# Decode attention for two problems on one core: the last rows of wo as one stripe in three pieces

## The chip, the cores and the metric

The kernel runs on one core of a Trainium2 chip. The metric is the device time of one execution in microseconds (us). The kernel before took 363.1 us (median of 3 runs, 363.03 to 363.24).

## The reference

Two independent problems, A and B, of the same shape. Each has 2 batches, one query token, 32 query heads on 16 key/value heads of 128 elements, and attends to the last 4096 of 16384 cached positions.

```python
q = (x @ wq).reshape(B, Sq, Hq, Dh)            # x 2x1x576, wq 576x4096
k = repeat(k_cache[:, :, Sk - W:, :], 2)       # W = 4096, Dh = 128
v = repeat(v_cache[:, :, Sk - W:, :], 2)
p = softmax(q k^T * Dh ** -0.5)
out = (p v).reshape(B, Sq, Hq * Dh) @ wo       # wo 4096x576
# result: concatenate([out_A, out_B], axis=-1), 2x1x1152, bf16
```

All inputs are bf16. Almost all of the bytes are the cached keys and values: 32 slabs of 4 MB.

## The kernel before, in words

**Stream.** All large loads go through SP's queue in one fixed order, written as the list `stream` (L322). A slab is the K or the V of one batch for four key/value heads: 128 partitions of 32 KB, each partition holding 128 keys (`KJ`) of 128 elements. There are 16 K slabs (K0 to K15) and 16 V slabs (V0 to V15); V comes three slabs behind K (`LAG`). They share a ring of four slots. A slot is loaded again when the last reader of its slab is done. The output matrix wo has a buffer of its own, `wob`, of 16 rows of 576 elements per partition.

**Groups.** Two slabs, one for each batch, make a group G of 4 key/value heads (0 to 7; 0 to 3 are problem A, `NG` is 8). For each group DVE transposes K (L436), TensorE makes the scores (L462 and L266, a helper that issues a matmul without loading weights), DVE, GpSimd and TensorE find the maxima, ScalarE takes the exponentials (L500), DVE transposes them (L509), TensorE multiplies by V (L539, 32 matmuls per slab, four at a time in four column groups), and DVE scales and folds the result (L562 to L569).

**Dg and pick.** What is left has to become the stationary side of the projection. `make_dg` (L573) spreads it over partitions by one fp32 matmul with a 0/1 matrix, and `make_pick` (L582) multiplies by a mask and sums over the entries that are zero but for one (L590 or L597, then L606). For groups 0 to 5 the 0/1 matrix is `selm`: an even group fills partitions 0 to 63 of `oM`, an odd one 64 to 127, so that two groups together make 16 sets of weights with all 128 partitions (16 rows of wo each, a stripe, called M0 to M2). For the last two groups, 6 and 7, the matrix is `selx` and the mask `cm16`: each group fills all 128 partitions of `oP` with 8 sets of weights, and each has 8 rows of wo of its own, called W6 and W7.

**Projection.** `make_projm` (L622) multiplies a stripe, `make_proj` (L645) the 8 rows of one of the last groups. For problem B each row is four matmuls of 144 columns (`cells`, L616): two column halves `c` by two halves `h`, the latter in two column groups of the array. The result is summed in PSUM (`PJ`).

**The end.** After the loop over the slabs (L741 to L770) the order on each engine is written out by hand. M2's 16 rows are multiplied in parts of 8, 4 and 4, put between other work. V15 is loaded in two parts, keys 0 to 79 and 80 to 127 (`v_cuts`, L160); the first part's matmuls run while the second is on its way. W6 comes in one DMA of 1152 KB, which waits for the first 8 rows of M2's projection; W7 in three, of 4, 3 and 1 rows (`w_cuts`, L162), which wait for all of M2's projection, since they go to the second half of `wob`. `filler` (L389) issues matmuls whose result nobody reads. Group 7's dg and pick are made for batch 0 (slab V14) and batch 1 (V15) apart. Then come W6's 8 rows, W7's rows 0 to 3, 4 to 6, and the last row, whose weights are loaded ahead (L654) and whose column half 0 is finished before half 1, so that DVE (L687) and ScalarE (L688) each evict one half and SP and ScalarE issue one output DMA each (L694).

The order at the end of the kernel before:

```python
        make_projm(NM - 1, 12, 16)
        filler(4)
        make_evac(i + 2)
        make_PV(i + 3, (0,))
        make_dg(NG - 1, (0,))
        make_pick(NG - 1, (0,))
        filler(4)
        make_PV(i + 3, (1,))
        make_evac(i + 3)
        filler(3)
        make_dg(NG - 1, (1,))
        make_pick(NG - 1, (1,))
        make_proj(NG - 2)
        make_proj(NG - 1)
        make_E(NPROB - 1)
```

Of the kernel before, what the change touches and what calls it, by code (L numbers as in the profile page):

```python
# [63 lines left out]
def build_kernel(nc, probs, out):  # L64
# [17 lines left out]
    KJ = W // 32  # L82
# [11 lines left out]
    with es:  # L94
# [21 lines left out]
        cm16 = sb("cm16", [128, 16], FP32)  # L116
        jmask_f = sb("jmask_f", [128, 8], FP32)
        m8 = sb("m8", [128, 16, 8], FP32)
        selx = sb("selx", [128, 8, 16], FP32)
# [13 lines left out]
        oP = sb("oP", [128, 2, 8, Bb], BF16)  # L133
        oM = sb("oM", [128, 16, Bb], BF16)
# [25 lines left out]
        v_cuts = [0, 80, KJ]  # L160
        lastv_sem = [sem("lastv")]
        w_cuts = [0, 4, 7, 8]  # L162
# [77 lines left out]
        d_cm = mask(cm16[:, 0:16], ident_f[:].rearrange("p (x q) -> p q x", q=16), AX.X, "cm16")  # L240
# [6 lines left out]
        p_sx = pool(lambda e: e.tensor_copy(selx[:], jmask_f[:, 0:8].unsqueeze(2).broadcast_to([128, 8, 16])), [d_jf], "selx")  # L247
# [83 lines left out]
        stream.append(("W", NG - 2))  # L331
        stream.append(("W", NG - 1))
        NM = NG // 2 - 1
# [13 lines left out]
        projm_first = {}  # L347

        def issue(key):
            kind, i = key  # L350
            if kind in "MW":
                n = 16 if kind == "M" else 8
                first_g = 2 * i if kind == "M" else i
                P, gl = first_g // GP, first_g % GP
                at = 0 if kind == "M" else 8 * (i % 2)
                rows = probs[P][4][gl * 1024:gl * 1024 + 128 * n, :].rearrange("(p j) n -> p j n", j=n)
                deps = ([projm_op[i - 1]] if i >= 1 else []) if kind == "M" else [projm_first[NM - 1] if i == NG - 2 else projm_op[NM - 1]]
                cuts = [(0, n, wo_sem[i % 2])]
                if i == NG - 1:
                    cuts = [(w_cuts[k], w_cuts[k + 1], ([wo_sem[1]] + lastw_sem)[k]) for k in range(3)]  # L360
                stream_dma[key] = []
                for j0, j1, sm in cuts:
                    def f(e, j0=j0, j1=j1, sm=sm):
                        return e.dma_start(wob[:, at + j0:at + j1, :].rearrange("p j n -> p (j n)"),
                                           rows[:, j0:j1, :].rearrange("p j n -> p (j n)")).then_inc(sm, 16)
                    stream_dma[key].append((j0, j1, dma_op("sp", sm, 1, f, deps, "wo%d_%d" % (i, j0))))
                return
            P, g, b = i // (2 * GP), (i // 2) % GP, i % 2
            src_t = probs[P][1] if kind == "K" else probs[P][2]
            src = src_t[b, 4 * g:4 * g + 4, Sk - W:Sk, :].rearrange("k (r j) d -> r k j d", j=KJ)  # L370
            r = slot_of[key]
            prior = uses[r][:uses[r].index(key)]
            deps = [last_reader[prior[-1]]] if prior else first_deps[r]
            cuts = [(0, KJ, ring_sem[r])]
            if key == ("V", NSLAB - 1):
                cuts = [(v_cuts[k], v_cuts[k + 1], ([ring_sem[r]] + lastv_sem)[k]) for k in range(2)]
            stream_dma[key] = []
            for c0, c1, sm in cuts:
                def f(e, c0=c0, c1=c1, sm=sm):
                    return e.dma_start(ring[:, r, c0 * 128:c1 * 128],  # L380
                                       src[:, :, c0:c1, :].rearrange("r k j d -> r k (j d)")).then_inc(sm, 16)
                stream_dma[key].append((c0, c1, dma_op("sp", sm, 1, f, deps, "%s%d_%d" % (kind, i, c0))))
# [23 lines left out]
        proj_op = {}  # L406
# [166 lines left out]
        def make_dg(G, bs=(0, 1)):  # L573
            b0, nb = bs[0], len(bs)
            sl_, p_sl = (selx, p_sx) if G >= NG - 2 else (selm, p_sm)
            n, bank, op = tb_job(lambda e, bank: e.matmul(bank[:, 0:128 * nb], sl_[:].rearrange("p h c -> p (h c)"),
                                                          oR[:, b0:b0 + nb, :].rearrange("p b d -> p (b d)"), start=True, stop=True),
                                 "dg%d_%d" % (G, b0), [ch[(G, "red%d" % b)] for b in bs] + [p_sl])
            ch[(G, "dg")] = op
            dg_job[(G, bs)] = (n, bank)  # L580

        def make_pick(G, bs=(0, 1)):  # L582
            v = G % 2
            b0, nb = bs[0], len(bs)
            n, bank = dg_job[(G, bs)]
            tv = tmp[:, 0:128 * nb]
            if G < NG - 2:
                h0 = 64 * v
                tv = tmp[h0:h0 + 64, 0:256]
                a = dve(lambda e: e.tensor_tensor(  # L590
                    tv.rearrange("p (b c j) -> p b c j", b=2, c=8), bank[h0:h0 + 64, 0:256].rearrange("p (b c j) -> p b c j", b=2, c=8),
                    jmask_f[h0:h0 + 64, 0:8].unsqueeze(1).unsqueeze(3).broadcast_to([64, 2, 8, 16]), ALU.mult),
                    [ch[(G, "dg")], d_jf, ch["tmp"]], "A%d" % G)
                dst, q = oM[h0:h0 + 64, :, :].rearrange("p j b -> p b j"), G // 2
                free, c = [projm_op[q - 1]] if q >= 1 else [], 8
            else:
                a = dve(lambda e: e.tensor_tensor(  # L597
                    tv.rearrange("p (b c j) -> p b c j", b=nb, c=16), bank[:, 0:128 * nb].rearrange("p (b c j) -> p b c j", b=nb, c=16),
                    cm16[:, 0:16].unsqueeze(1).unsqueeze(3).broadcast_to([128, nb, 16, 8]), ALU.mult), [ch[(G, "dg")], d_cm, ch["tmp"]], "A%d" % G)
                dst = oP[:, v, :, b0:b0 + nb].rearrange("p j b -> p b j")  # L600
                free, c = [], 16
            tb_consumer[n] = a

            def f_pick(e):
                with nc.allow_low_precision(reason="one term of the c is not zero"):
                    return e.tensor_reduce(dst, tv.rearrange("p (b c j) -> p b j c", b=nb, c=c), AX.X, ALU.add)  # L606
            ch[(G, "oP", b0)] = dve(f_pick, [a] + free, "oP%d_%d" % (G, b0))
            ch["tmp"] = ch[(G, "oP", b0)]
# [12 lines left out]

        def make_projm(q, j0=0, j1=16):  # L622
            P, start = 2 * q // GP, (2 * q) % GP == 0 and j0 == 0
            ensure(("M", q))
# [13 lines left out]
            deps = [ch[(2 * q, "oP", 0)], ch[(2 * q + 1, "oP", 0)], stream_dma[("M", q)][0][2]]  # L638
            if start:
                deps += [e_ops[(P - 1, 0)], e_ops[(P - 1, 1)]] if P >= 1 else [q_ev[2]]  # L640
            projm_op[q] = pe(f, deps, "projm%d_%d" % (q, j0))
            if j0 == 0:
                projm_first[q] = projm_op[q]

        def make_proj(G):  # L645
            v = G % 2
            ensure(("W", G))
            oPs = [ch[(G, "oP", b)] for b in range(2) if (G, "oP", b) in ch]
            for j0, j1, dma in stream_dma[("W", G)]:
                held = G == NG - 1 and j1 == 8  # L650
                if held:
                    def f_w(e):
                        for h in range(2):
                            last = e.add_instruction(mybir.InstLdweights(  # L654
                                name=nc.get_next_instruction_name(), engine=mybir.EngineType.PE,
                                ins=[e.lower_ap(oP[:, v, 7, :], for_matmul_weights=True)], outs=[],
                                tile_size=(128, 32), tile_position=(0, 32 * h)))
                        return last
                    pe(f_w, oPs, "projw%d" % G)

                    for c in range(2):
                        def f_c(e, c=c):
                            for h in range(2):
                                last = cell(e, oP[:, v, 7, :], 8 * v + 7, c, h, False, True)
                            return last
                        last_cell[c] = pe(f_c, oPs + [dma], "proj%d_7%d" % (G, c))
                    continue

                def f(e, j0=j0, j1=j1):
                    for j in range(j0, j1):  # L670
                        last = cells(e, oP[:, v, j, :], 8 * v + j, False)
                    return last
                proj_op[G] = pe(f, oPs + [dma], "proj%d_%d" % (G, j0))

        def make_E(P):
# [7 lines left out]
            for h in range(2):  # L683
                def f_first(e, h=h):
                    return e.dma_start(out[:, 0, h * NH:(h + 1) * NH], out_sb[:, h * NH:(h + 1) * NH]).then_inc(out_sem, 16)
                dma_op(("sp", "act")[h], out_sem, 1, f_first, [e_ops[(0, 0)], e_ops[(0, 1)], stream_dma[("W", NG - 1)][1][2]], "out0_%d" % h)
# [61 lines left out]
        make_projm(NM - 1, 0, 8)  # L748
        make_dg(NG - 2)
        make_projm(NM - 1, 8, 12)  # L750
# [5 lines left out]
        make_projm(NM - 1, 12, 16)  # L756
# [5 lines left out]
        filler(4)  # L762
# [5 lines left out]
        make_proj(NG - 2)  # L768
        make_proj(NG - 1)
# [93 lines left out]
```

## Time and profile before

| what | value |
|---|---|
| time, median of 3 runs | 363.1 us |
| time of the profiled execution | 363.1 us |
| its span (first to last instruction) | 361.8 us |
| bytes read from HBM | 153.10 MB, 423 GB/s over the span |
| busy: TensorE (PE), DVE, ScalarE (ACT), GpSimd (POOL) | 229.0, 218.6, 45.4, 24.3 us |
| mean granted clock of TensorE | 0.887 of full speed |
| last V matmul, second part of V15 | issued from 354.20 us on |
| W6's first row, W7's first row, last row | 357.10, 358.50, 359.82 us |
| evictions, output DMAs issued | 360.10 and 360.15, 360.46 and 360.47 us |

Times inside the execution are counted from the start of the span. The profiled execution took 1.3 us more than its span. In a timeline line the first number is the start, the second the duration, then engine, line, operation, output and inputs, count, and in brackets the idle time before it with what ended it. PEld is the loading of weights, SPq and ACTq are the issue of a DMA.

### The profile page before, as it was taken

The numbers are of one execution on the slowest core, as the hardware profiler recorded it, in microseconds if no ns is written. First come the engines' busy times: TensorE is split into PE (matmuls) and PEld (weight loads), VectorE is DVE, ScalarE is ACT, GpSimd is POOL, SyncE is SP. The second block draws the span as 40 slices with busy tenths as digits, with TensorE's granted clock in tenths as the row PEclk, the third lists the DMA queues.
The fourth block names the chain that finished last, engine by engine and source line by source line (L and its number), as shares of the span: only waits on it lengthen the run. The fifth ranks groups of instructions, "written<-read, shape, count | busy, mean of one in ns | idle before, by whom it ended". The sixth has DMA issues, their size and how long they took to land.

```text
span 361.8 us, 2701 instructions
## 1 busy us (share of the span) xinstructions
PE 229.0 (63%) x1357; PEld 56.1 (16%) x943; DVE 218.6 (60%) x150; ACT 45.4 (13%) x77; POOL 24.3 (7%) x84
## 2 busy tenths in 40 slices
PE   0397687767464866671696656662776675667575
PEld 0010111112110211120121211110112121112222
DVE  0811898495949392924919493952927776675522
ACT  1002100040031002200005000500005000500500
POOL 4200101100010001000010000000010000001000
PEclk9999698969999889888798998899589897869989
DMA  8999999999999999999999999999999999999996
GB/s 327 449 428 420 442 426 424 446 413 446 417 447 420 442 422 422 439 438 420 438 424 434 431 438 412 448 420 442 424 435 429 428 438 420 434 442 420 427 417 258
DMA packets 6088, 153.28 MB, mean 424 GB/s; under 512 B 684, under 2 KB 828, under 8 KB 1084
## 3 DMA queue, kind: packets, MB, share of 16 engines
q1 hardware_dynamic: 6056, 153.10, 98.7%
q8 instruction: 9, 0.15, 0.2%
q14 instruction: 3, 0.02, 0.0%
q10 hardware_dynamic: 20, 0.01, 0.0%
HBM read 153.10 MB, written 0.00 MB: 423 GB/s over the span
## 4 chain that ended last, share of the span: by engine, by line
DMA 49%; DVE 24%; PE 16%; issue 8%; ACT 1%; POOL 1%; SPq 0%
DMA ring<-in_B_k_cache_dram 25%; DVE xt L436 15%; DMA ring<-in_B_v_cache_dram 9%; DMA ring<-in_B_wq_dram 7%; DMA ring<-in_A_k_cache_dram 6%; PE st L266 6%; PE st L462 5%; DMA wob<-in_B_wo_dram 3%; DVE oR L569 2%; DVE mx L470 2%; DVE pT L509 2%; PE pj L266 2%; DVE tmp L562 2%; PE ot L539 1%; ACT pR L500 1%
## 5 line engine op out<-in xcount | busy, mean ns | idle before, releaser
L462 PE MATMUL st<-xt,zq 128*128 128x512 bf16 x256 | 119.3, 466 | 93.6 <-DVE xt L436 93.6
L436 DVE STREAM_TRANSPOSE xt<-ring 128x4096 f32<-128x4096 f32 x32 | 141.6, 4429 | 33.5 <-DMA ring<-in_A_k_cache_dram 18.2
L266 PE MATMUL st<-xt,zq 128*128 128x512 bf16 x256 | 118.0, 461 | 0.0
L500 ACT ACTIVATE pR<-st,bias 128x512 bf16<-128x512 f32 x32 | 40.0, 1419 | 219.0 <-DVE bias L493 219.0
L462 PEld LDWEIGHTS st<-xt,zq 128*128 128x128 bf16 x256 | 28.3, 110 | 211.5 <-DVE xt L436 110.0
L539 PE MATMUL ot<-ring,pT 128*32 128x512 bf16 x512 | 32.0, 393 | 8.3 <-DMA ring<-in_B_v_cache_dram 8.3
L493 DVE SCALAR_TENSOR_TENSOR bias<-vmask,tb,offm 128x4 f32<-128x4 f32 x8 | 1.8, 224 | 37.1 <-PE tb L490 37.1
L523 DVE TENSOR_REDUCE ssum<-tb 128x2 f32<-128x8 f32 x8 | 1.3, 162 | 33.4 <-PE tb L520 33.4
L428 POOL TENSOR_TENSOR zq<-qs,bmask 128x64 bf16<-128x64 bf16 x32 | 8.6, 292 | 161.2 <-PE st L266 140.3
L509 DVE STREAM_TRANSPOSE pT<-pR 128x2048 bf16<-128x2048 bf16 x8 | 18.4, 2303 | 0.7 <-ACT pR L500 0.7
L562 DVE SCALAR_TENSOR_TENSOR tmp<-ot,rsb,dmask 128x512 f32<-128x512 f32 x16 | 11.5, 719 | 9.4 <-PE ot L539 9.4
L281 PE MATMUL ot<-ring,pT 128*32 128x512 bf16 x18 | 7.6, 421 | 15.1 <-DMA ring<-in_A_wq_dram 14.5
L539 PEld LDWEIGHTS ot<-ring,pT 128*32 128x32 bf16 x512 | 12.4, 99 | 23.7 <-DMA ring<-in_B_v_cache_dram 10.5
L569 DVE TENSOR_REDUCE oR<-tmp 128x128 f32<-128x512 f32 x15 | 15.6, 1039 | 0.5
L266 PE MATMUL pj<-ring,pT 128*32 128x512 bf16 x36 | 12.1, 422 | 0.0
L266 PE MATMUL pj<-wob,oM 128*2 128x288 bf16 (+1 forms) x64 | 10.2, 256 | 0.0
L470 DVE TENSOR_REDUCE mx<-st 128x2 f32<-128x1024 f32 x8 | 9.7, 1208 | 0.1
L500 ACT ACTIVATION_READ_ACCUMULATOR pR<-st,bias 128x1 f32 x32 | 9.1, 283 | 0.0
L636 PE MATMUL pj<-wob,oM 128*2 128x288 bf16 x32 | 7.9, 286 | 0.0
L224 DVE TENSOR_TENSOR xt<-xt,hmask 4x1152 bf16<-4x1152 bf16 x2 | 2.8, 1398 | 8.4 <-DMA xt<-in_A_x_dram 8.4
L266 PE MATMUL st<-ring,pT 128*32 128x512 bf16 x18 | 7.4, 414 | 0.0
L472 POOL TENSOR_TENSOR mv<-mx,v 128x2 f32<-128x2 f32 x8 | 1.6, 195 | 80.0 <-DVE mx L470 80.0
(71 smaller groups left out, 79.5 us busy)
## 6 DMA issues: line engine op xcount, KB each, us to landing
ring<-in_A_k_cache_dram SPq DMA_DIRECT2D x8, 4096.0 KB, 24.9
ring<-in_A_v_cache_dram SPq DMA_DIRECT2D x8, 4096.0 KB, 30.0
ring<-in_B_k_cache_dram SPq DMA_DIRECT2D x8, 4096.0 KB, 28.5
ring<-in_B_v_cache_dram SPq DMA_DIRECT2D x7, 4096.0 KB, 31.8
ring<-in_A_wq_dram SPq DMA_DIRECT2D x1, 4608.0 KB, 13.6
ring<-in_B_wq_dram SPq DMA_DIRECT2D x1, 4608.0 KB, 24.1
wob<-in_A_wo_dram SPq DMA_DIRECT2D x2, 2304.0 KB, 29.8
ring<-in_B_v_cache_dram SPq DMA_DIRECT2D x1, 2560.0 KB, 26.9
```

The lines of the kernel that those rows point to most:

```text
L266: return e.add_instruction(mybir.InstMatmult(name=nc.get_next_instruction_name(), engine=mybir.EngineType.PE, ins=[e.lower_ap(mv_), e.lowe ...
L281: last = e.matmul(QB[c], wt, mv_, start=first, stop=True, skip_group_check=True)
L428: last = e.tensor_tensor(dst, src, msk, ALU.mult)
L436: Xop[(t, jh)] = dve(lambda e: e.transpose(xt[:, jh, :].bitcast(FP32).rearrange("p (kp x kt) -> p x kp kt", kp=2, kt=2), ring[:, r, jh * H ...
L462: last = e.matmul(ob, wt, mv_, start=first, stop=True, skip_group_check=True)
L470: ch[(G, "max")] = dve(lambda e: e.tensor_reduce(mx[:], st[:, :].rearrange("p (x t) -> p t x", t=2), AX.X, ALU.max), [Sop[(2 * G + 1, 1)]] ...
L500: last = e.activation(pR[:].rearrange("p (x k) -> p k x", k=4)[:, kv, :], st[:, :].rearrange("p (x t) -> p t x", t=2)[:, kv % 2, :], ACTF.Exp,
L509: pT_op[G] = dve(lambda e: e.transpose(pT[:, v, :].rearrange("p (w j q) -> p j w q", w=4, q=8), pR[:].rearrange("p (j w q) -> p j w q", w= ...
L539: last = e.matmul(OTB[32 * c:32 * c + 32, :], pT[:, v, base + 32 * c:base + 32 * c + 32], ring[:, r, jj * 128:(jj + 4) * 128], start=rd == ...
L562: evac_op[i] = dve(lambda e: e.scalar_tensor_tensor(tv, o, rsb[:, v, b:b + 1], dm, ALU.mult, ALU.mult), deps, "ev%d" % i)
L569: ch[(G, "red%d" % b)] = dve(lambda e: e.tensor_reduce(oR[:, b, :], tmp[:].rearrange("p (j d) -> p d j", j=4), AX.X, ALU.add), [evac_op[i] ...
L636: last = e.matmul(PJ[0], oM[:, j, :], mv_, start=start and j == 0, stop=True, skip_group_check=True)
```

## The change

- Groups 6 and 7 are picked like all others, with `selm` and the 64-partition form, into the halves of one set of weights; `selx`, `cm16` and `oP` go, and with them one copy on GpSimd and one reduction on DVE near the start.
- wo's last 16 rows per partition are one stripe M3 in three DMAs of 12, 3 and 1 rows (1728, 432 and 144 KB). Each piece waits for the rows of M2 that it overwrites: the first for M2's rows up to 12, the others for all of M2.
- `oM` has two buffers, by the parity of the stripe; a pick waits for the projection two stripes back.
- The projection of the last 16 rows, in groups of 12, 3 and 1, stands behind the last pick; every group waits for all picks of groups 6 and 7 and for its own piece.
- V15 is divided at key 96 instead of 80: parts of 3072 and 1024 KB, 24 and 8 matmuls.
- Fillers: 2 instead of 4 between the two parts of V15, and 4 new ones between group 7's last dg and the projection.

The diff, cut to its core:

```diff
-        oP = sb("oP", [128, 2, 8, Bb], BF16)
-        oM = sb("oM", [128, 16, Bb], BF16)
+        oM2 = [sb("oM%d" % k, [128, 16, Bb], BF16) for k in range(2)]
...
-        v_cuts = [0, 80, KJ]
+        v_cuts = [0, 96, KJ]
-        w_cuts = [0, 4, 7, 8]
+        m_cuts = [0, 12, 15, 16]
...
-        d_cm = mask(cm16[:, 0:16], ident_f[:].rearrange("p (x q) -> p q x", q=16), AX.X, "cm16")
...
-        p_sx = pool(lambda e: e.tensor_copy(selx[:], jmask_f[:, 0:8].unsqueeze(2).broadcast_to([128, 8, 16])), [d_jf], "selx")
...
-        stream.append(("W", NG - 2))
-        stream.append(("W", NG - 1))
-        NM = NG // 2 - 1
+        NM = NG // 2
+        stream.append(("M", NM - 1))
...
-                deps = ([projm_op[i - 1]] if i >= 1 else []) if kind == "M" else [projm_first[NM - 1] if i == NG - 2 else projm_op[NM - 1]]
-                cuts = [(0, n, wo_sem[i % 2])]
-                if i == NG - 1:
-                    cuts = [(w_cuts[k], w_cuts[k + 1], ([wo_sem[1]] + lastw_sem)[k]) for k in range(3)]
+                cuts = [(0, 16, wo_sem[i % 2])]
+                if i == NM - 1:
+                    cuts = [(m_cuts[k], m_cuts[k + 1], ([wo_sem[1]] + lastw_sem)[k]) for k in range(3)]
...
+                    deps = [projm_rows[i - 1][j1]] if i >= 1 else []
...
-            sl_, p_sl = (selx, p_sx) if G >= NG - 2 else (selm, p_sm)
...
+            h0, q = 64 * v, G // 2
+            tv = tmp[h0:h0 + 64, 0:128 * nb]
+            a = dve(lambda e: e.tensor_tensor(
+                tv.rearrange("p (b c j) -> p b c j", b=nb, c=8), bank[h0:h0 + 64, 0:128 * nb].rearrange("p (b c j) -> p b c j", b=nb, c=8),
+                jmask_f[h0:h0 + 64, 0:8].unsqueeze(1).unsqueeze(3).broadcast_to([64, nb, 8, 16]), ALU.mult),
+                [ch[(G, "dg")], d_jf, ch["tmp"]], "A%d_%d" % (G, b0))
+            dst = oM2[q % 2][h0:h0 + 64, :, b0:b0 + nb].rearrange("p j b -> p b j")
+            free = [projm_rows[q - 2][16]] if q >= 2 else []
...
             deps = [ch[(2 * q, "oP", 0)], ch[(2 * q + 1, "oP", 0)], stream_dma[("M", q)][0][2]]
+            if q == NM - 1:
+                deps = oPs_last() + [dma for c0, c1, dma in stream_dma[("M", q)] if c0 <= j0 and j1 <= c1]
...
-        make_projm(NM - 1, 12, 16)
+        make_projm(NM - 2, 12, 16)
         filler(4)
         make_evac(i + 2)
         make_PV(i + 3, (0,))
         make_dg(NG - 1, (0,))
         make_pick(NG - 1, (0,))
-        filler(4)
+        filler(2)
         make_PV(i + 3, (1,))
         make_evac(i + 3)
         filler(3)
         make_dg(NG - 1, (1,))
         make_pick(NG - 1, (1,))
-        make_proj(NG - 2)
-        make_proj(NG - 1)
+        filler(4)
+        make_projm(NM - 1, 0, 12)
+        make_projm(NM - 1, 12, 15)
+        make_last_row()
         make_E(NPROB - 1)
```

`make_last_row` is the last row's part of the old `make_proj`, with row 15 of the stripe and `oM`'s weights: load the weights ahead, then column half 0, then half 1.

More of the change, by code (lines that the diff above doesn't have):

```diff
@@ L115, in build_kernel @@
         dmask = sb("dmask", [128, 4], FP32)
-        cm16 = sb("cm16", [128, 16], FP32)
         jmask_f = sb("jmask_f", [128, 8], FP32)
         m8 = sb("m8", [128, 16, 8], FP32)
-        selx = sb("selx", [128, 8, 16], FP32)
         selm = sb("selm", [128, 16, 8], FP32)
@@ L346, in build_kernel @@
         projm_op = {}
-        projm_first = {}
+        projm_rows = {}
         def issue(key):
             kind, i = key
[L351 to L356, printed above, removed]
-                deps = ([projm_op[i - 1]] if i >= 1 else []) if kind == "M" else [projm_first[NM - 1] if i == NG - 2 else projm_op[NM - 1]]
-                cuts = [(0, n, wo_sem[i % 2])]
-                if i == NG - 1:
-                    cuts = [(w_cuts[k], w_cuts[k + 1], ([wo_sem[1]] + lastw_sem)[k]) for k in range(3)]
+            if kind == "M":
+                P, gl = 2 * i // GP, 2 * i % GP
+                rows = probs[P][4][gl * 1024:gl * 1024 + 2048, :].rearrange("(p j) n -> p j n", j=16)
+                cuts = [(0, 16, wo_sem[i % 2])]
+                if i == NM - 1:
+                    cuts = [(m_cuts[k], m_cuts[k + 1], ([wo_sem[1]] + lastw_sem)[k]) for k in range(3)]
                 stream_dma[key] = []
@@ L363, in f @@
                     def f(e, j0=j0, j1=j1, sm=sm):
-                        return e.dma_start(wob[:, at + j0:at + j1, :].rearrange("p j n -> p (j n)"),
+                        return e.dma_start(wob[:, j0:j1, :].rearrange("p j n -> p (j n)"),
                                            rows[:, j0:j1, :].rearrange("p j n -> p (j n)")).then_inc(sm, 16)
+                    deps = [projm_rows[i - 1][j1]] if i >= 1 else []
                     stream_dma[key].append((j0, j1, dma_op("sp", sm, 1, f, deps, "wo%d_%d" % (i, j0))))
@@ L405, in build_kernel @@
         evac_op = {}
-        proj_op = {}
         last_cell = {}
@@ L574, in make_dg @@
             b0, nb = bs[0], len(bs)
-            sl_, p_sl = (selx, p_sx) if G >= NG - 2 else (selm, p_sm)
-            n, bank, op = tb_job(lambda e, bank: e.matmul(bank[:, 0:128 * nb], sl_[:].rearrange("p h c -> p (h c)"),
+            n, bank, op = tb_job(lambda e, bank: e.matmul(bank[:, 0:128 * nb], selm[:].rearrange("p h c -> p (h c)"),
                                                           oR[:, b0:b0 + nb, :].rearrange("p b d -> p (b d)"), start=True, stop=True),
-                                 "dg%d_%d" % (G, b0), [ch[(G, "red%d" % b)] for b in bs] + [p_sl])
+                                 "dg%d_%d" % (G, b0), [ch[(G, "red%d" % b)] for b in bs] + [p_sm])
             ch[(G, "dg")] = op
@@ L585, in make_pick @@
             n, bank = dg_job[(G, bs)]
[L586 to L601, printed above, removed]
+            h0, q = 64 * v, G // 2
[6 more added lines that the diff above has]
+            free = [projm_rows[q - 2][16]] if q >= 2 else []
             tb_consumer[n] = a
@@ L605, in f_pick @@
                 with nc.allow_low_precision(reason="one term of the c is not zero"):
-                    return e.tensor_reduce(dst, tv.rearrange("p (b c j) -> p b j c", b=nb, c=c), AX.X, ALU.add)
+                    return e.tensor_reduce(dst, tv.rearrange("p (b c j) -> p b j c", b=nb, c=8), AX.X, ALU.add)
             ch[(G, "oP", b0)] = dve(f_pick, [a] + free, "oP%d_%d" % (G, b0))
@@ L620, in cells, with oPs_last @@
             return last
+        def oPs_last():
+            return [ch[(G, "oP", b)] for G in (NG - 2, NG - 1) for b in range(2) if (G, "oP", b) in ch]
         def make_projm(q, j0=0, j1=16):
             P, start = 2 * q // GP, (2 * q) % GP == 0 and j0 == 0
+            oM = oM2[q % 2]
             ensure(("M", q))
@@ L641, in make_projm @@
             projm_op[q] = pe(f, deps, "projm%d_%d" % (q, j0))
[L642 to L671, printed above, removed]
@@ new lines, in make_projm, with make_last_row, f_w, f_c @@
+            for k in range(j0 + 1, j1 + 1):
+                projm_rows.setdefault(q, {})[k] = projm_op[q]
+        def make_last_row():
+            q = NM - 1
+            oM = oM2[q % 2]
+            def f_w(e):
+                for h in range(2):
+                    last = e.add_instruction(mybir.InstLdweights(
+                        name=nc.get_next_instruction_name(), engine=mybir.EngineType.PE,
+                        ins=[e.lower_ap(oM[:, 15, :], for_matmul_weights=True)], outs=[],
+                        tile_size=(128, 32), tile_position=(0, 32 * h)))
+                return last
+            pe(f_w, oPs_last(), "projw")
+            for c in range(2):
+                def f_c(e, c=c):
+                    for h in range(2):
+                        last = cell(e, oM[:, 15, :], 15, c, h, False, True)
@@ L672, in f @@
                     return last
-                proj_op[G] = pe(f, oPs + [dma], "proj%d_%d" % (G, j0))
+                last_cell[c] = pe(f_c, oPs_last() + [stream_dma[("M", q)][2][2]], "proj15_%d" % c)
         def make_E(P):
@@ L685, in f_first @@
                     return e.dma_start(out[:, 0, h * NH:(h + 1) * NH], out_sb[:, h * NH:(h + 1) * NH]).then_inc(out_sem, 16)
-                dma_op(("sp", "act")[h], out_sem, 1, f_first, [e_ops[(0, 0)], e_ops[(0, 1)], stream_dma[("W", NG - 1)][1][2]], "out0_%d" % h)
+                dma_op(("sp", "act")[h], out_sem, 1, f_first, [e_ops[(0, 0)], e_ops[(0, 1)], stream_dma[("M", NM - 1)][1][2]], "out0_%d" % h)
             evs = [dve(lambda e: e.tensor_copy(out_w[:, 0:NQ], PJW[0]), [last_cell[0]], "E%d_0" % P),
@@ L747, in build_kernel @@
         make_evac(i + 1)
-        make_projm(NM - 1, 0, 8)
+        make_projm(NM - 2, 0, 8)
         make_dg(NG - 2)
-        make_projm(NM - 1, 8, 12)
+        make_projm(NM - 2, 8, 12)
         make_pick(NG - 2)
```

## The prediction

> **What bounds the kernel now.** I read the slices of the page first, then the chain that ended last, then the DMA issues and the timeline of the last 12 us, and last the busy time by clock window. First the page: share of the 16 DMA engines and GB/s in 40 slices of 9 us.
>
> ```profile
> DMA  8999999999999999999999999999999999999996
> GB/s 327 449 428 420 442 426 424 446 413 446 417 447 420 442 422 422 439 438 420 438 424 434 431 438 412 448 420 442 424 435 429 428 438 420 434 442 420 427 417 258
> ```
>
> Only the first and the last slice have room: the kernel is one stream of 153 MB, and only the start and the end can move. The end is on the chain (start us, us, what):
>
> ```profile
> 348.51 10.90 DMA wob<-in_B_wo_dram
> 359.41 0.04 issue
> 359.45 0.23 PE pj L614 x2
> ...
> 360.13 0.02 issue
> 360.15 0.28 ACT out_w L688
> ```
>
> The last-but-one piece of wo lands at 359.41, its three rows follow 0.04 us later, then the last row, the eviction and the two output DMAs. So PE has almost nothing left to do when the stream ends. The last pieces of the stream (KB, then us from issue to landing):
>
> ```profile
> ring<-in_B_v_cache_dram SPq DMA_DIRECT2D x1, 2560.0 KB, 26.9
> ring<-in_B_v_cache_dram SPq DMA_DIRECT2D x1, 1536.0 KB, 30.0
> wob<-in_B_wo_dram SPq DMA_DIRECT2D x1, 1152.0 KB, 19.4
> wob<-in_B_wo_dram SPq DMA_DIRECT2D x1, 576.0 KB, 10.2
> wob<-in_B_wo_dram SPq DMA_DIRECT2D x1, 432.0 KB, 10.9
> wob<-in_B_wo_dram SPq DMA_DIRECT2D x1, 144.0 KB, 10.8
> ```
>
> With the issues in SP's timeline (323.59, 324.2, 337.54, 348.13, 348.51, 349.0) they land at 350.5, 354.2, 356.94, 358.33, 359.41 and 359.8. The two largest gaps give the price of the stream: 1152 KB in 2.74 us and 576 KB in 1.39 us, 2.4 ns per KB. Now PE behind them:
>
> ```profile
> 350.51 1.26 PE L539 MATMUL ot<-ring,pT 128*32 128x512 bf16 x20 [1.45 <-DMA ring<-in_B_v_cache_dram]
> ...
> 354.20 0.83 PE L539 MATMUL ot<-ring,pT 128*32 128x512 bf16 x12 [1.14 <-DMA ring<-in_B_v_cache_dram]
> ...
> 357.10 0.23 PE L614 MATMUL pj<-wob,oP 128*2 128x144 bf16 x2
> ...
> 358.03 0.23 PE L266 MATMUL pj<-wob,oP 128*2 128x144 bf16 x2
> 358.47 0.43 PEld L614 LDWEIGHTS pj<-wob,oP 128*2 128x2 bf16 x8 [0.47 <-issue]
> 358.50 0.23 PE L614 MATMUL pj<-wob,oP 128*2 128x144 bf16 x2 [0.24 <-DMA wob<-in_B_wo_dram]
> ```
>
> The reader is to see that the first eight rows (group 6, whose pick was done long before) run from 357.10 to 358.1, while their successor's stripe is still in flight. Rows start at 358.50, 358.62, 358.75, 358.87: 0.124 us per row of four matmuls.
>
> **The change, part by part.**
>
> *Bytes and DMAs.* The same 2304 KB of wo come as 1728, 432 and 144 KB instead of 1152, 576, 432 and 144; the last V slab as 3072 and 1024 KB instead of 2560 and 1536. Nothing is added to the stream. The 1728 KB land when the 576 KB did, 358.33, less what one DMA costs by itself. That cost is not a row: from 1152 to 576 KB the price per KB is equal (saving 0); the 432 KB took 1.08 us against 1.04 at 2.4 ns per KB, so 0.04; twice that, 0.1, is my far end. I take 0.05 us: landing 358.28. The later pieces move with it.
>
> *SP's queue.* The 1728 KB wait for row 12 of the stripe before, not row 8: issued after PE's rows at 339.08 to 339.6 instead of at 337.54. What is queued behind it on SP waited for the rows at 347.44 to 348.0 anyway. At 340 the queue still holds over 14 us of work (354.2 lands before it), so the later issue is covered; if that cover were gone it would cost its 2.1 us.
>
> *Projection.* This is the term that counts. Groups 6 and 7 share one stripe, so each row's weights are half from each group and no row can start before the last pick. Eight rows that ran in the shadow (357.10 to 358.1) now stand behind it, and behind the landing of the 1728 KB. The landing is the later of the two (pick below). Before: rows 0-3 at 358.50, a wait of 0.29 us, rows 4-6 at 359.45, the last row at 359.82, DVE's eviction at 360.10. After: first row 0.15 us behind the landing (today's 576 KB: 358.50 against 358.33, 0.17; the 432 KB: 359.45 against 359.41, 0.04; the first is nearer, since it too waits for two semaphores): 358.43. Sixteen rows without a gap: the last starts 15 x 0.124 = 1.87 us later, 360.30. The pieces of 432 and 144 KB (359.36, 359.7) land while PE is in rows 7 to 10 and stop nothing. Eviction 0.28 us behind the last row's start, as now: 360.58 against 360.10, **+0.48**. Two more waits on semaphores that are long up: between the three rows and the last one today the pitch stays 0.06 us per pair, so 0; up to 0.1 each if PE can't look ahead.
>
> *Last V slab.* 512 KB more in the first part: it lands 512 x 2.4 ns = 1.23 us later, 351.7. The second ends where it did, 354.2, with 8 matmuls behind it instead of 12: 4 x 0.054 (20 in 1.26 us, less the 0.2 that a last one takes to drain) = 0.21 us less. The pick today ends at 357.53 + 0.39 = 357.92, so then 357.71, 0.6 us ahead of the landing: worth nothing.
>
> *Picks.* They go from 128 partitions (L597 292 ns, L606 386 ns for 128 elements) to 64 partitions with 16 outputs of 8 instead of 8 of 16. For 256 elements the two forms stand at 422 and 582 ns against 425 and 612: equal. No cost, and 0.6 us of cover.
>
> *Fillers.* Two fewer between the parts of V, four more behind the last dg. dg starts at 356.47, dg and the four take 0.42 + 4 x 0.216 us, to about 357.8 (0.42 us is today's step from 356.68 to the row at 357.10, 0.216 a filler's share of three in 0.81 us, less drain): covered by the wait for 358.3. Masks: one 128x16 reduce on DVE and one copy on POOL go from the start, where both wait for wq anyway: 0, and 0.3 us at most. The second oM buffer takes a wait away that was never late: 0.
>
> Sum: 0.48 less rounding and the DMA's 0.04 margin, **+0.45 us**. The profiled execution took 363.1 us (span 361.8, 1.3 around it), which is also the median of the runs shown. So 363.55 us, +0.12%. A measurement of this kernel can tell about 0.2% (0.73 us) from no change, so this is "same". Ends for this case alone: 363.3 (first row sooner, smaller pitch) to 363.8 (both waits cost 0.1, landing as today).
>
> **Rivals.**
>
> *The clock falls in the longer wait (slower).* PE waits 1.45 us for the first V part; then 2.68 (349.07 to 351.74). The granted clock stands on a grid of 3.41 us. Columns: PE busy, PEld, DVE, ACT, POOL, granted clock, DMA, GB/s.
>
> ```profile
> 319.75:323.16 3.41, 1.08 (x5) 0.10 (x1) 3.41 (x1) 0.00 (x0) 0.00 (x0) 1.00 1.03 442
> 323.16:326.58 3.42, 2.96 (x7) 0.54 (x4) 0.40 (x1) 0.00 (x0) 0.00 (x0) 0.50 0.96 412
> ...
> 347.06:350.47 3.41, 2.01 (x32) 0.48 (x13) 1.78 (x2) 0.00 (x0) 0.00 (x0) 1.00 1.00 424
> 350.47:353.88 3.41, 2.54 (x26) 0.76 (x23) 0.68 (x2) 0.00 (x0) 0.00 (x0) 1.00 0.98 414
> ```
>
> A window with 1.08 us of PE (also 1.42 at 145.67) is followed by one at half clock; one with 1.50 (142.26) or 2.01 is not. On this trace's grid the changed kernel is safe: up to 350.47 nothing differs (2.01), and 350.47 to 353.88 still holds about 2.2. But one trace does not tie the grid to the kernel's start. A window brings the clock down if 1.93 us or more of the 2.68 lie in it, which is so for boundaries from 351.0 to 353.2, two thirds of all positions; and only where the half clock then reaches V's second part does it cost. Half clock is priced by the V matmuls from 344.41: 32 in 3.19 us, most of them at 0.50, 0.107 us each. Boundary at 352.0: 0.73 us busy before it; 19 of the 24 matmuls at 0.107 us end at 354.05, dg 0.64 and two fillers 0.85 (both ahead of V's second part on PE) reach 355.5, then 8 matmuls, eviction from 356.1 instead of 354.9, pick at 358.95, the rows from 359.05, the last at 360.92: +1.10, 364.2. At 351.0 and 353.0 the same steps give +0.8 and +0.5. So 363.9 to 364.4 for about a third of all positions (where the half clock lies between 351.0 and 352.2, or a little beyond); it decides when the pick ends after 358.3. Against it: the fillers, and this trace's grid.
>
> The Trainium skill (TensorE: Matmul & The Clock Gate, Part 1) says that the gate falls after a whole idle window of about 3.4 us. By that rule a wait of 2.68 us would leave the clock alone, and the time would be 363.55 at every position. The rows above speak against it: 1.08 us of work in the window did not keep the clock. The same section calls the window free-running, which one trace can't show.
>
> *The projection stays hidden (no change).* If the 1728 KB land 0.4 us sooner, the end is the landing of the last piece, 359.8, as now: 363.1. For it: each DMA less is work less on the slowest engine; against it: 0.04 us measured, ten times too little. Chance small.
>
> *Faster by over 0.2%.* The stream would have to end 0.7 us sooner with equal bytes; only a DMA engine that happens to be less delayed gives that: 362.3.
>
> **How the numbers follow.** Forecast 0.58 (363.55), clock 0.30 (364.2), hidden 0.09 (363.1), faster 0.03 (362.3). Predicted: 363.55. Range 363.1 to 364.3: below it the faster case, above it the worst positions of the clock. Slower by over 0.2% (above 363.83): the clock's 0.28 and 0.06 of the forecast's upper end, 0.34. Faster 0.03. Same 0.63.
>
> **What would show it.** First row of wo about 0.15 us behind the landing of the 1728 KB, near 358.4; sixteen rows at 0.124 without a gap; DVE's eviction near 360.6 with no wait for a wo DMA on the chain after the first row. A pick past 358.3 and a granted clock of 0.50 between 351 and 356 would show the clock. I am wrong if the pick, not the landing, starts the rows at full clock, if rows take another pitch, or if a landing moves by more than 0.2 us.

## The result and the profile after

The changed kernel takes 363.6 us (median of 22 executions, 363.35 to 364.41) against 363.12 us (22 executions, 362.97 to 363.34): ratio 1.0017, 95% interval 1.0011 to 1.0024. The medians differ by 0.48 us, 0.13%; forecast were 0.45 us. But the 22 times of the changed kernel are two groups with a gap between: 14 from 363.35 to 363.71 (median 363.49) and 8 from 363.95 to 364.41 (median 364.12). The kernel before has one group, 0.37 us wide. The forecast is the lower group, the clock rival the upper one, and the profiled execution of the changed kernel, at 364.4 us (span 363.2), is one of the upper.

The page's slices of that execution: the stream is as full as before, and only the last slice has more room.

```profile
DMA  8999999999999999999999999999999999999994
GB/s 325 447 430 415 451 415 446 419 440 426 437 428 426 440 423 418 447 422 444 419 437 425 433 433 421 440 430 433 430 433 431 433 430 419 442 437 426 428 414 191
```

The chain of the changed kernel (start us, us, what) no longer ends with a wo DMA. From V15's first part to the eviction, it is TensorE and DVE alone:

```profile
322.60 29.23 DMA ring<-in_B_v_cache_dram
351.88 2.50 PE ot L529 x24
354.38 0.73 PE tb L565 x2
355.11 0.43 PE st L383
355.53 0.31 PE st L261
355.85 0.57 PE ot L529 x8
...
359.38 0.16 PE pj L595 x2
361.29 0.20 PE pj L261 x6
361.51 0.28 ACT out_w L665
```

Two fillers (L383, L261) stand on the chain, ahead of V15's second part. Its windows, on the grid of this execution's clock (PE busy, PEld, DVE, ACT, POOL, granted clock, DMA, GB/s):

```profile
348.77:352.18 3.41, 1.11 (x12) 0.20 (x12) 0.56 (x1) 0.00 (x0) 0.00 (x0) 1.00 0.92 388
352.18:355.60 3.42, 3.42 (x28) 1.08 (x19) 0.42 (x2) 0.00 (x0) 0.00 (x0) 0.50 1.05 444
355.60:359.01 3.41, 2.52 (x18) 0.53 (x12) 2.12 (x6) 0.00 (x0) 0.00 (x0) 1.00 0.75 304
```

The boundary at 352.18 has 1.11 us of work in the window before it, and half clock behind it, just where V15's first part and the two fillers run. The same in the timeline of the changed kernel:

```profile
351.88 2.50 PE L529 MATMUL ot<-ring,pT 128*32 128x512 bf16 x24 [2.30 <-DMA ring<-in_B_v_cache_dram]
...
355.77 0.62 PE L529 MATMUL ot<-ring,pT 128*32 128x512 bf16 x8
...
358.89 0.37 DVE L587 TENSOR_REDUCE oM<-tmp 64x16 bf16<-64x128 f32 x1
359.31 1.78 PEld L595 LDWEIGHTS pj<-wob,oM 128*2 128x2 bf16 x30 [0.96 <-DVE oM L587]
...
361.46 0.30 DVE L664 CAST out_w<-pj 34x144 bf16<-34x144 f32 x1 [2.21 <-PE pj L261]
```

V15's second part begins at 355.77, not when it lands at 354.3, the pick ends at 359.26, and the bracket of the weights' line names the pick, not a DMA, as what the rows waited for. The joined piece was issued at 341.66 and took 16.8 us:

```profile
wob<-in_B_wo_dram SPq DMA_DIRECT2D x1, 1728.0 KB, 16.8
```

So it lay ready from about 358.5 on, 0.8 us before the pick ended, and is not late. Eviction is at 361.46 against 360.10: 1.36 us later, about what the two profiled times differ by (364.4 and 363.1).

### The profile page after: what moved, and what is told of

Same layout as the page of the kernel before. It is cut to its first block, busy times and chain, and to the rows that moved or that the text cites. A ratio compares the mean times of both kernels' runs of the same rounds, so it can differ in the third digit from the quotient of the medians.

```text
span 363.2 us, 2701 instructions
## 1 busy us (share of the span) xinstructions
PE 231.1 (64%) x1359; PEld 56.8 (16%) x944; DVE 218.0 (60%) x149; ACT 45.5 (13%) x77; POOL 24.2 (7%) x83
## 4 chain that ended last, share of the span: by engine, by line
DMA 48%; DVE 31%; PE 12%; issue 6%; ACT 1%; POOL 0%; SPq 0%; DVEq 0%
DMA ring<-in_B_k_cache_dram 24%; DVE xt L426 20%; DMA ring<-in_A_k_cache_dram 16%; DMA ring<-in_B_v_cache_dram 8%; PE st L452 4%; PE st L261 4%; DVE pT L499 2%; DVE oR L559 2%; DVE mx L460 2%; DVE tmp L552 2%; PE pj L261 1%; ACT pR L490 1%; PE pj L621 1%; PE ot L529 1%; DVE oM L587 1%
## 5 line engine op out<-in xcount | busy, mean ns | idle before, releaser
L426 DVE STREAM_TRANSPOSE xt<-ring 128x4096 f32<-128x4096 f32 x32 | 141.4, 4427 | 30.8 <-DMA ring<-in_A_k_cache_dram 16.8
L261 PE MATMUL st<-xt,zq 128*128 128x512 bf16 x256 | 117.5, 459 | 0.0
L529 PE MATMUL ot<-ring,pT 128*32 128x512 bf16 x512 | 34.4, 414 | 8.8 <-DMA ring<-in_B_v_cache_dram 6.2
L276 PE MATMUL ot<-ring,pT 128*32 128x512 bf16 x18 | 7.3, 407 | 16.1 <-DMA ring<-in_A_wq_dram 14.6
L261 PE MATMUL pj<-wob,oM 128*2 128x144 bf16 (+1 forms) x98 | 12.9, 256 | 0.0
L261 PE MATMUL pj<-ring,pT 128*32 128x512 bf16 x36 | 11.6, 407 | 0.0
L565 PE MATMUL tb<-oR,selm 128*128 128x256 f32 (+1 forms) x18 | 6.2, 427 | 3.2 <-DVE ssum L513 1.5
L577 DVE TENSOR_TENSOR tmp<-tb,jmask_f 64x256 f32<-64x256 f32 (+1 forms) x9 | 3.5, 394 | 7.4 <-PE tb L565 7.2
```

What stands on the lines that cost most here:

```text
L261: return e.add_instruction(mybir.InstMatmult(name=nc.get_next_instruction_name(), engine=mybir.EngineType.PE, ins=[e.lower_ap(mv_), e.lowe ...
L276: last = e.matmul(QB[c], wt, mv_, start=first, stop=True, skip_group_check=True)
L426: Xop[(t, jh)] = dve(lambda e: e.transpose(xt[:, jh, :].bitcast(FP32).rearrange("p (kp x kt) -> p x kp kt", kp=2, kt=2), ring[:, r, jh * H ...
L529: last = e.matmul(OTB[32 * c:32 * c + 32, :], pT[:, v, base + 32 * c:base + 32 * c + 32], ring[:, r, jj * 128:(jj + 4) * 128], start=rd == ...
```

## The experiments

Theory: two costs. At full clock the landing of the twelve rows starts sixteen rows that have no shadow (lower group); where the grid falls badly, the wait of 2.3 to 2.7 us ahead of V15's first part halves the clock and delays the pick beyond that landing (upper group). Rivals: a late landing makes the upper group; the waits or the new pick make the 0.4 us. Each edit is of the changed kernel unless it says otherwise.

**Nine fillers ahead of V15's first part.**

```diff
         make_projm(NM - 2, 12, 16)
-        filler(4)
+        filler(9)
```

> The changed kernel with nine fillers instead of four ahead of V15's first part, so that TensorE waits about 1.5 us there instead of 2.3 to 2.7. Theory (the clock falls in that wait in some executions, and the rows behind the landing cost 0.45 us in all): the upper group of times (364.0 to 364.4, 8 of 22 executions of the changed kernel) goes, the lower one stays: all executions between 363.3 and 363.8. Rival (the upper group comes from a landing that is late, not from the clock): about a third of the executions stays above 363.9.

11 executions, 363.30 to 363.59, median 363.39; before beside it 363.06; ratio 1.0010 (1.0002 to 1.0019). The upper group is gone. This is also the trace of the forecast's own case (the changed kernel with nine fillers):

```profile
351.61 1.48 PE L529 MATMUL ot<-ring,pT 128*32 128x512 bf16 x24 [1.18 <-DMA ring<-in_B_v_cache_dram]
...
354.10 0.62 PE L529 MATMUL ot<-ring,pT 128*32 128x512 bf16 x8 [0.16 <-DMA ring<-in_B_v_cache_dram]
...
357.21 0.37 DVE L587 TENSOR_REDUCE oM<-tmp 64x16 bf16<-64x128 f32 x1
358.29 1.80 PEld L595 LDWEIGHTS pj<-wob,oM 128*2 128x2 bf16 x30 [1.62 <-DVE oM L587]
358.32 0.23 PE L595 MATMUL pj<-wob,oM 128*2 128x144 bf16 x2 [0.62 <-DMA wob<-in_B_wo_dram]
...
360.46 0.30 DVE L664 CAST out_w<-pj 34x144 bf16<-34x144 f32 x1 [2.89 <-PE pj L261]
```

The pick ends at 357.58; the first matmul's bracket names the wo DMA, 0.74 us later; sixteen rows follow without a gap, and eviction is at 360.46, 0.36 us behind that of before.

**V15 divided at key 80 again.**

```diff
-        v_cuts = [0, 96, KJ]
+        v_cuts = [0, 80, KJ]
```

> The changed kernel with V15 divided at key 80 as before; all else as changed, with two fillers between the parts. Theory: the first part lands at 350.5 again, TensorE waits 1.45 us, the clock stays up, and the landing of the 1728 KB still starts the sixteen rows: one group of times, 363.4 to 363.7. Rival (the later landing of V's first part costs by itself, or the landing of wo is late): either 363.1, or still a third of the executions above 363.9.

11 executions, 363.28 to 363.84, median 363.51 (ratio 1.0013, 1.0004 to 1.0021): one group without a third of its executions above 363.9, though wider at both ends than the 363.4 to 363.7 that were stated. In its trace V15's first part starts at 350.40 after a wait of 1.42 us, and the rows at 358.33 behind the wo DMA. So the upper group comes from the division, and the lower group's cost does not.

**V15 divided at key 112.**

```diff
-        v_cuts = [0, 96, KJ]
+        v_cuts = [0, 112, KJ]
```

> The changed kernel with V15 divided at key 112: the first part lands at about 352.9, TensorE waits 3.9 us ahead of it, 28 matmuls in the first part and 4 in the second. Theory: the half clock falls on the first part at every position of the clock's grid, so the lower group of times goes: 364.0 to 365.5 in all executions, the rows behind a pick at 359 to 360. Rival (the clock has no part in it): the last pick is earlier, since only 4 matmuls follow the last landing, and the time is 363.5 in two thirds of the executions as before.

6 executions: 363.93, 365.02, 365.29, 365.49, 366.13, 366.17. Nothing is left at 363.5; one execution lies 0.07 us below the stated 364.0, and two go beyond the stated end of 365.5. The windows of the profiled one, with the wait in the first:

```profile
349.27:352.68 3.41, 0.78 (x3) 0.00 (x0) 0.51 (x1) 0.00 (x0) 0.00 (x0) 1.00 0.87 363
352.68:356.10 3.42, 3.27 (x29) 1.12 (x29) 0.00 (x0) 0.00 (x0) 0.00 (x0) 0.50 1.03 432
```

A smaller last part of V is worth nothing when the wait ahead of the larger one halves the clock. The half clock is shown for the profiled execution, 365.29; for the others it is inferred from their times, and why two reach 366.1 and not 365.5 was not traced.

**wo's last stripe in four pieces.**

```diff
-        m_cuts = [0, 12, 15, 16]
+        m_cuts = [0, 8, 12, 15, 16]
...
-        make_projm(NM - 1, 0, 12)
+        make_projm(NM - 1, 0, 8)
+        make_projm(NM - 1, 8, 12)
```

> The changed kernel with wo's last stripe in four pieces of 8, 4, 3 and 1 rows instead of 12, 3 and 1, and the projection in the same groups. Theory: in executions at full clock the first rows start behind the pick at 357.8 instead of the landing of 12 rows at 358.3, sixteen rows are through by 359.8, and the end is the last landing again: 363.1 in about two thirds of the executions; the others, where the pick comes at 359, stay at 364.0 to 364.4. Rival (the 0.45 us come from the waits on three semaphores, or from the new pick): the lower group stays at 363.5.

11 executions: seven from 363.01 to 363.19, four from 364.14 to 364.37. The lower group is back at the time of before, the upper one untouched. The profiled execution is one of the lower. It waits 2.29 us ahead of V15's first part, as long as the upper group's execution shown above (2.30), but its clock's grid lies elsewhere, the window ahead holds 1.50 us of TensorE's work instead of 1.11, and the clock stays up:

```profile
347.74:351.15 3.41, 1.50 (x23) 0.35 (x7) 1.78 (x2) 0.00 (x0) 0.00 (x0) 1.00 0.91 387
351.15:354.57 3.42, 2.73 (x36) 0.99 (x35) 0.66 (x2) 0.00 (x0) 0.00 (x0) 1.00 1.00 417
```

The rows in the trace of the four pieces:

```profile
357.71 1.40 PEld L595 LDWEIGHTS pj<-wob,oM 128*2 128x2 bf16 x24 [0.96 <-DVE oM L587]
...
359.45 0.28 PEld L595 LDWEIGHTS pj<-wob,oM 128*2 128x2 bf16 x6 [0.33 <-DMA wob<-in_B_wo_dram]
...
360.09 0.30 DVE L664 CAST out_w<-pj 34x144 bf16<-34x144 f32 x1 [2.44 <-PE pj L261]
```

Twelve rows are through before the piece of three lands, as in the kernel before (eight of W6, four of W7). So the stripe with its one projection is not what costs: the size of its first piece is.

**Both repairs.** Four pieces and nine fillers.

> The changed kernel with both repairs: nine fillers ahead of V15's first part and wo's last stripe in four pieces of 8, 4, 3 and 1 rows. Theory (two separate costs, the clock and the landing of twelve rows): one group of times, 363.0 to 363.3, level with the kernel before. Rival (a third cost is left in the one projection behind the last pick): 363.3 to 363.6.

11 executions, 362.88 to 363.27, median 363.08 against 363.06: ratio 1.0001 (0.9992 to 1.0009). No third cost is left, and no gain either: the chain that ended last goes through the landing of the three rows' piece in both, at 359.54 here and at 359.41 before. No version here beats the kernel before.

**The kernel before with V15 divided at 96** and two fillers between its parts.

```diff
-        v_cuts = [0, 80, KJ]
+        v_cuts = [0, 96, KJ]
...
         make_pick(NG - 1, (0,))
-        filler(4)
+        filler(2)
```

> The kernel before with only V15's division at key 96 and two fillers instead of four between its parts. Theory: the half clock falls on V15's first part in about a third of the executions here too and the pick ends near 359.3, but only W7's eight rows stand behind it, so these come at 363.4 to 363.6 and the others at 363.0 to 363.2. Rival (the clock's cost needs the single stripe): one group at 363.1.

11 executions: seven from 362.89 to 363.18, four from 363.38 to 363.51. The division brings the second group without the stripe too, 0.4 us above the first. With the stripe the second group has its median at 364.12, 0.7 us above this one's 363.40. Eight more rows behind the late pick would be 8 x 0.124 = 1.0 us; the 0.3 us between are not explained by a trace, since the profiled execution here is one of the lower group. A part may be W6's eight rows, which TensorE here does between the last dg and W7's rows; that is argued, not shown.

**Nine fillers, and none behind the last dg.**

```diff
         make_projm(NM - 2, 12, 16)
-        filler(4)
+        filler(9)
...
         make_pick(NG - 1, (1,))
-        filler(4)
```

> The changed kernel with nine fillers ahead of V15's first part and without the four fillers behind the last dg. Theory (those four lie in the wait for the landing and a wait of 1.5 us keeps the clock): as with nine fillers alone, 363.3 to 363.6. Rival (they are needed to hold the clock for the sixteen rows): rows at 0.24 us instead of 0.124 in some executions, 364.5 to 365.5.

6 executions: 363.51, 363.53, 363.58, and 364.83, 364.99, 365.05. The theory fails for half of them, which come where the rival put them: these four fillers are needed. The next run looks for how.

**No filler at all behind V15's second part.**

```diff
         make_evac(i + 3)
-        filler(3)
```

on top of the last edit.

> The changed kernel with nine fillers ahead of V15's first part and with none behind its second part: neither the four behind the last dg nor the three ahead of it, so that TensorE does 0.5 us of work between 354.8 and 358.4. Theory (half of the executions without the four fillers ran their sixteen rows at half clock): now all do, rows at 0.245 us instead of 0.124 for most of the stripe, 364.8 to 365.6 in every execution, with a granted clock of 0.50 under the rows in the trace. Rival (the four fillers helped in another way, such as the loading of code or weights ahead): rows at 0.124 in the trace and two groups of times as without the four.

3 executions: 364.54, 365.20, 365.54, the first 0.3 us below what was stated. Windows of the profiled one (365.2), then lines of its timeline:

```profile
353.08:356.50 3.42, 1.62 (x13) 0.52 (x13) 2.13 (x5) 0.00 (x0) 0.00 (x0) 1.00 1.00 423
356.50:359.91 3.41, 2.04 (x31) 1.13 (x17) 0.66 (x2) 0.00 (x0) 0.00 (x0) 0.50 0.53 209
```

```profile
358.24 3.36 PEld L595 LDWEIGHTS pj<-wob,oM 128*2 128x2 bf16 x30 [1.63 <-DVE oM L587]
...
362.19 0.30 DVE L664 CAST out_w<-pj 34x144 bf16<-34x144 f32 x1 [4.55 <-PE pj L261]
```

The 30 weight loads take 3.36 us instead of 1.80: the stripe runs at half clock, with the first row at 358.27, as early as ever. The window ahead holds 1.62 us of TensorE's work, more than the 1.50 that kept the clock in the trace of the four pieces, so how much is enough has no sharp edge here. The trace shows the half clock for this kernel; that the upper three executions of the last experiment had the same is inferred from their time, since its profiled execution was one of the lower three.

**No fillers between V15's parts.**

```diff
         make_pick(NG - 1, (0,))
-        filler(2)
```

> The changed kernel without the two fillers between V15's parts. Theory (at half clock these two, queued ahead of V15's second part, take 0.85 us of the delay of the pick): the lower group stays at 363.35 to 363.7, the upper comes down from 364.0 to 364.4 to about 363.4 to 363.8, so that no execution is above 363.9. Rival (the first part's matmuls at half clock alone make the delay): a third of the executions stays above 363.9.

11 executions: eight from 363.36 to 363.64, then 363.80, 363.80 and 363.95. The upper three have come down by 0.3 us (median 363.80 against 364.12), not wholly into the lower group: the two fillers, meant to hold the clock, made a part of the delay when the clock was down. On the chain of the upper group's trace they stand with 0.74 us; that the time gains less, and that the rest is V15's first part itself, is inferred, since the profiled execution here is one of the lower. One execution lies 0.05 us above the line that was drawn.

## Why the prediction was right, step by step

*The sum.* Forecast 363.55, measured 363.6. That the median comes so near is in part luck: the lower group, which is the forecast's case, is at 363.49, 0.37 us above before for a sum of 0.45, and the eight executions of the upper group move the median up to 363.6. The terms themselves stood. From V15's second part to the first row it is 358.32 - 354.10 = 4.22 us with the joined piece, and 358.50 - 354.20 = 4.30 before: the first row gains 0.08 us, where 0.07 were worked out (358.43 against 358.50). To the eviction it is 6.36 us against 5.90, so the tail is 0.46 us longer, where 0.48 were worked out. The last step from 0.48 to 0.45 takes the saving of a DMA, which is already in the landing at 358.28, a second time. In this trace the eviction comes only 0.36 us later because V15's second part begins 0.10 us earlier; in the traces without the late pick it begins anywhere from 354.03 to 354.31, and why was not traced. The rest stood too: rows at 0.124 us without a gap (358.32 to the eviction at 360.46 is 2.14 us for 1.87 + 0.28 worked out), no cost of the added waits, none of the 64-partition pick (0.37 us against 0.39).

*What decides.* The pick ahead of the landing at full clock: 357.58 against 357.7 worked out, and the DMA in the bracket. The four pieces show that the landing is the cause: with a smaller, earlier first piece the lower group went back to 363.1.

*The clock.* Given 0.30 and 363.9 to 364.4; 8 of 22 executions came, from 363.95 to 364.41. The worked example (boundary at 352.0, pick at 358.95, rows from 359.05, 364.2) is close to the profiled execution (boundary at 352.18, pick at 359.26, rows from 359.31, 364.4); there V15's first part began 0.14 us later and its dg at 354.31 instead of 354.05. That the grid is not tied to the kernel's start shows now: its boundaries stand at 350.47 in the trace of before, at 352.18 in this one and at 352.68 with key 112. The edge between 1.42 and 1.50 us of work, on which the third of all positions rests, is not as sharp as the prediction has it: in the trace of before a window with 1.56 us (from 261.72) is followed by half clock too. The range, 363.1 to 364.3, held the median and cut off the top two executions.

By the rule of the Trainium skill that was weighed (TensorE: Matmul & The Clock Gate, Part 1: cold after a whole idle window) there would have been no upper group. The rows decide against it: 1.11 us of work in a window of 3.41 did not keep the clock.

*What was missed.* The four new fillers were priced at nothing because the wait for the landing covers them. That is true, but not all of it: the prediction did not ask what the wait would do without them, though the same rule answers it, since PE then waits 0.9 us for dg and 1.5 us for the landing within one window. They are worth 1.4 us in half of the executions. The small terms that were set to zero (masks, the second oM buffer) were not tried one by one; both repairs together leave 0.02 us for all of them. SP's later issue is not among these, since the first of the four pieces waits for row 8 again; with nine fillers alone the joined piece was issued at 341.30 instead of 337.54, and its first row still came 0.08 us sooner behind V15's second part than before.

## What to carry to other kernels

When a stage ends on a landing, ask which work could be done before that landing and no longer can: a joined load saves 0.08 us here and takes eight rows, 1.0 us, out of the shadow, and dividing the same stripe more finely gives all of it back. When a division is moved, price the wait ahead of it as well as the work behind it: a wait of 2.5 us cost more than four matmuls saved, and only in a third of the executions, so that a single profile, or three runs, may show either case. In these runs fillers paid ahead of a wait and cost time ahead of work that was late, and a filler's worth is what the next burst costs without it.

## What the runs showed of the hardware that was not expected

The times of one and the same program fell into two groups, 0.6 us apart in the changed kernel, with 8 of 22, 4 of 11, 4 of 11 and 3 of 11 executions in the upper one, near the third of the grid's positions that the prediction had worked out. That the half clock can hit either of two places of one tail (V15's first part, or the stripe) was seen only when the fillers were taken away.
